# Local attention with memory and two MLPs on one core: slices of MLP 1's second weights in one tile and one request, values in two requests, and other places for loads and for the preparation of MLP 2's weights

## The chip, the cores and the metric

The kernel runs on one core of a Trainium2 chip. TensorE (PE in the rows) multiplies, and its weight loads (PEld) run beside the products. VectorE (DVE), ScalarE (ACT) and GpSimd (POOL) do the element-wise work. The DMA requests that matter here are issued by SyncE (SP) in the order in which its program lists them. The metric is the device time of one launch in microseconds (us).

## The reference

```python
# attention: batch 4, 8 heads, 768 positions, 64 per head; chunks of 32 queries
for c in range(24):
    k_full = concat([mem_k, k[chunk - 16 left : chunk + 8 right]])   # 8 memory keys + window
    v_full = concat([mem_v, v[same window]])
    out[chunk] = softmax(q[chunk] @ k_full.T / 8) @ v_full
x = out as [3072 tokens, 512]
# MLP 1: w_in [512, 2048], w_out [2048, 512]
h = x @ w_in;  g = h - tanh(h);  x = g @ w_out
# MLP 2: same shapes, other weights
h = x @ w_in
g = where(h >= 1, h, where(h <= -1, 0, (h + 1)**2 / 4));  out = g @ w_out
```

All inputs and the result are float32.

## The kernel before

**Number format.** Each float32 operand of a large product is split into a high and a low part in TensorE's own 32-bit format (fp32r), and three products are summed: high·high, low·high, high·low. So every weight slice exists twice, as `whi` and `wlo`, and every activation slice as `ghi` and `glo`. ScalarE makes a high part with a copy, VectorE the low part with a subtraction.

**Blocks.** The 3072 tokens are six blocks of 512 columns. The 2048 hidden units are sixteen slices (`FC`) of 128. A step `s` is one block and one slice: block `s // 16`, slice `s % 16`. `hidden(s)` (L706) makes `h` from twelve products of 512 columns, `gate(s)` (L716, L717) makes `g = h - tanh(h)`, and `output(s)` (L746) adds twelve products into the four banks of `acc` (two tiles, `acc0` and `acc1`, of two banks each). After a block's sixteen slices the four banks are copied to `y` (ScalarE copies `acc0`, VectorE copies `acc1`, L757) and stored in DRAM. The last two blocks run together in `both` (L784).

**Attention** is done in groups of eight chunks (`a`, L516 and L592), spread between the steps. Queries of a group come in one request, keys `k` in four, values `v` in four (L500).

**Weights of MLP 1.** They are loaded as float32 into `stage` (L159), rounded by ScalarE, VectorE and GpSimd, and split. The split second weights are written to DRAM once (`w1o_store`, L225, `hi` and `lo` apart) and read again for each later block (`w1o_load`, L234, also apart). Four pairs of tiles (`whi1_0` to `whi1_3` and the `lo` ones) take them in turn; blocks 2 and 3 use six homes.

**Weights of MLP 2** are prepared beside MLP 1: sixteen pieces (two weights, eight pieces each) pass through load, rounding (`prep_act`, L247 and L248, on ScalarE, then `prep_mag`, `prep_sign` and `prep_add` on VectorE), differences of quarters (`prep_sums`, L283, on VectorE), copies of the high parts (`prep_hi`, L297 and L310, on ScalarE), low parts (`prep_lo`, L316, on VectorE) and stores. `prep_items` lists these as items with a cost; `work(c)` is called after each product or step, adds `c` to a credit, and pops items until the credit is used up. So the costs and credits set at which product an item is issued.

**MLP 2's first layer** is done by Strassen's scheme in three parts of two blocks each (`early_plan(-2)`, `early_plan(-1)` and a last one). A product (`product`, L1069) is summed in PSUM in `qa`, `qb` or `qc`, and the results are combined through copies `u` and `v` (L972, ScalarE) and additions (L982, L1002, L1009, VectorE). A bank is used again only after its copy or addition has read it. The parts of weights that the products read come in requests at L961, ten of them ahead into homes named in the list `IN`.

**The order of the work** is a schedule written by hand: step `i` runs the lists `before`, `rounds`, `inside`, `between` and `behind`, and each engine executes its instructions in the order in which the program issues them. The stretches of the span are: the start to 48 us; hidden slices of block 0 to 107; outputs of blocks 0 and 1 to 258; `early_plan(-2)` to 342; outputs of blocks 2 and 3 to 457; `early_plan(-1)` to 535; `both` to 623; the last Strassen part of the first layer to 707; MLP 2's second layer (L1156) and what is left of the first to the end.

**SP's lanes.** Each request uses one of eight completion semaphores in turn (`DMAHW0` to `DMAHW7` in the kernel's order), and SP waits until that lane's request before has landed, so at most eight requests are under way.

Of the kernel before, what the change touches and what calls it, by code (L numbers as in the profile page):

```python
# [30 lines left out]
KC = DM // 128  # L31
# [48 lines left out]
def tile_memory_attention_two_mlps(  # L80
# [17 lines left out]
    att = ctx.enter_context(tc.tile_pool(name="att", bufs=2))  # L98
    ps_h = ctx.enter_context(tc.tile_pool(name="ps_h", bufs=2, space=PSUM))
# [100 lines left out]
    split_t = {}  # L200

    def split_weights_hi(s, which):
        phase, b, fc = steps[s]
        r = raw_t[phase, which, fc]
        hi = slot(f"whi{which}_{s % (W1O if which else 2)}", f"whi{which}_{s}", F32R)
# [3 lines left out]
    def split_weights_lo(s, which):  # L209
        phase, b, fc = steps[s]  # L210
        r, hi = raw_t[phase, which, fc], split_t[s, which]
        lo = slot(f"wlo{which}_{s % (W1O if which else 2)}", f"wlo{which}_{s}", F32R)
# [10 lines left out]
    def w1o_store(s):  # L223
        for i, t in enumerate(split_t[s, 1]):
            nc.sync.dma_start(out=w1o_d[steps[s][2]][:, i, :], in_=t.bitcast(F32))  # L225

    W1O_LATE = ("1_0", "1_1", "0_0", "0_1", "1_2", "1_3")

    def w1o_load(s):
        if s < PLAIN + FC:  # L230
            n = W1O_LATE[(s - NH) % 6] if NH <= s < PLAIN else f"1_{s % W1O}"
            t = [slot(f"w{w}{n}", f"w{w}1_{s}", F32R) for w in ("hi", "lo")]
            for i in range(2):
                nc.sync.dma_start(out=t[i].bitcast(F32), in_=w1o_d[steps[s][2]][:, i, :])  # L234
            split_t[s, 1] = t
# [160 lines left out]
    def prep_items():  # L396
# [8 lines left out]
        for n, p in enumerate(PAIRS):  # L405
# [6 lines left out]
                (1.4, [(load, n + 1, 0), (load, n + 1, 1), (prep_hi, *p, 0), (prep_sums, *p)]),  # L412
# [41 lines left out]
    def att_load(t, keys=True, values=True):  # L454
# [275 lines left out]
    def output(s):  # L730
# [80 lines left out]
    def retire(*tags):  # L811
# [6 lines left out]
        (-2, 7): ("whi1_2", "wlo1_2", "whi1_3", "wlo1_3"),  # L818
# [3 lines left out]
    def x_parts(sb, i):  # L822
        home = XHOME.get(i)
        name = f"xc{i}_{sb}"
        if (sb, i) in EARLY_HOME:
            home = EARLY_HOME[sb, i]
            if len(home) == 2:
                a = [wide.tile([128, 2, N], F32R, tag=tag, name=f"{name}_{k}") for k, tag in enumerate(home)]
# [549 lines left out]
    temps = ["ghi1", "glo1", "g14", "g15", "whi1_1", "wlo1_1"] + [f"y{i}" for i in range(KC)]  # L1378
# [132 lines left out]
```

## Time and profile before

| | us |
|---|---|
| median of three runs | 1094.72 |
| lowest and highest of them | 1092.56 and 1095.43 |
| the profiled execution | 1092.54 |
| its span (first to last instruction) | 1090.4 |
| around the span | 2.1 |

The profile's rows are one execution. A row of the timeline gives the start, the length, the engine, the line of the kernel, the operation, the tile written and the tile read, and, in brackets, how long the engine had been idle and what released it. A `q` behind an engine (SPq) is its sequencer, which issues requests. "PEclk" in a table by stretch is TensorE's granted clock as a share of 2.4 GHz (0.50 is 1.2 GHz), "DMA share" the mean busy share of the sixteen DMA engines.

### The profile page before, as it was taken

The page shows a single profiled execution, that of the slowest core. Times are in us where ns is not written, and L with a number is a line of the kernel's source. Part 1 is how long each engine was busy: PE and PEld are TensorE (multiplying, and loading weights), DVE is VectorE, ACT ScalarE, POOL GpSimd, SP SyncE. Part 2 cuts the span into 40 slices and gives each one's busy share as a digit, 9 for nine tenths or more (in the row PEclk, how much of TensorE's full clock was granted, in tenths as well). Part 3 has the DMA queues.
Part 4 walks back from the last instruction along what each step waited for, and adds up shares of the span by engine and source line. Part 5 has one row for each costly group of instructions (what it writes and reads, how often), then busy time and mean ns, then how long its engine had stood idle before and what let it go on. Part 6 is the DMA issues. An engine that isn't in the chain of part 4 may idle for free.

```text
span 1090.4 us, 20699 instructions
## 1 busy us (share of the span) xinstructions
PE 1050.5 (96%) x7535; PEld 849.1 (78%) x7541; DVE 821.7 (75%) x1384; ACT 639.6 (59%) x1164; POOL 42.6 (4%) x38
## 2 busy tenths in 40 slices
PE   7799999999889999999999999999999999999998
PEld 3577888777668877788788787788888888888887
DVE  4898978768887555677879988888567788476854
ACT  3588666436554332466546677756477756477653
POOL 0232221000000000000000000000000000000000
PEclk9899999999999999999999999999999999999999
DMA  9998986987867989799999898887866787767774
GB/s 215 257 258 223 263 234 200 281 235 247 279 230 211 265 242 283 271 325 344 375 342 297 282 362 280 261 265 217 250 195 192 224 260 220 226 194 194 202 204 147
DMA packets 218612, 274.01 MB, mean 251 GB/s; under 512 B 65808, under 2 KB 127504, under 8 KB 218512
## 3 DMA queue, kind: packets, MB, share of 16 engines
q1 hardware_dynamic: 218368, 272.57, 82.3%
q8 instruction: 60, 0.98, 0.4%
q14 instruction: 40, 0.33, 0.1%
q10 hardware_dynamic: 144, 0.13, 0.0%
HBM read 207.62 MB, written 65.01 MB: 250 GB/s over the span
## 4 chain that ended last, share of the span: by engine, by line
PE 81%; DVE 6%; DMA 5%; ACT 4%; SPq 3%; issue 1%; DVEq 0%; ACTq 0%
PE acc L1156 21%; PE acc L746 14%; PE qa L1069 10%; PE both L784 8%; PE h L706 7%; PE qc L1069 5%; PE qb L1069 2%; SPq L487 1%; PE a L592 1%; DMA stage<-w_in 1%; PE a L516 1%; DMA whi<-w1o 1%; SPq L500 1%; DMA wlo<-w1o 1%; ACT t L986 1%
## 5 line engine op out<-in xcount | busy, mean ns | idle before, releaser
L1156 PE MATMUL acc<-ghi,inG 128*128 128x512 f32 x672 | 183.0, 389 | 0.0
L288 DVE TENSOR_TENSOR glo<-g,ghi 128x512 fp32r<-128x512 f32 x194 | 130.0, 685 | 29.7 <-ACT ghi L287 27.9
L287 ACT ACTIVATE ghi<-g 128x512 fp32r<-128x512 f32 x194 | 118.6, 628 | 53.4 <-PE acc L1156 22.1
L1156 PEld LDWEIGHTS acc<-ghi,inG 128*128 128x128 f32 x672 | 126.2, 188 | 26.3
L1069 PE MATMUL qa<-xc,inP 128*128 128x512 f32 x576 | 141.2, 391 | 3.7 <-ACT u L972 2.5
L1069 PEld LDWEIGHTS qa<-xc,inP 128*128 128x128 f32 x576 | 107.3, 188 | 29.6 <-ACT u L972 5.5
L1156 PE MATMUL acc<-glo,inG 128*128 128x512 f32 x336 | 107.0, 389 | 0.0
L746 PE MATMUL acc<-ghi,whi 128*128 128x512 f32 x256 | 75.1, 406 | 5.3 <-DMA whi<-w1o 3.3
L1156 PEld LDWEIGHTS acc<-glo,inG 128*128 128x128 f32 x336 | 63.0, 188 | 13.4 <-DVE glo L288 0.5
L1069 PE MATMUL qc<-xc,inP 128*128 128x512 f32 x288 | 73.1, 389 | 0.0
L746 PE MATMUL acc<-ghi,wlo 128*128 128x512 f32 x256 | 70.9, 391 | 0.7 <-DMA wlo<-w1o 0.7
L746 PE MATMUL acc<-glo,whi 128*128 128x512 f32 x256 | 70.7, 390 | 0.0
L986 ACT ACTIVATE t<-g,half 128x512 f32<-128x512 f32 x58 | 42.0, 725 | 45.1 <-DVE g L982 45.1
L1069 PEld LDWEIGHTS qc<-xc,inP 128*128 128x128 f32 x288 | 54.0, 188 | 11.2
L746 PEld LDWEIGHTS acc<-ghi,whi 128*128 128x128 f32 x256 | 45.2, 188 | 16.5 <-DMA whi<-w1o 3.0
L746 PEld LDWEIGHTS acc<-ghi,wlo 128*128 128x128 f32 x256 | 47.9, 188 | 11.9 <-DMA wlo<-w1o 1.6
L987 ACT ACTIVATE t<-t 128x512 f32<-128x512 f32 x87 | 55.0, 632 | 2.8
L746 PEld LDWEIGHTS acc<-glo,whi 128*128 128x128 f32 x256 | 48.0, 188 | 10.5 <-issue 0.3
L194 POOL TENSOR_TENSOR raw<-raw,stage 128x512 int32<-128x512 int32 x32 | 41.9, 1309 | 144.1 <-DVE raw L189 88.5
L990 DVE SCALAR_TENSOR_TENSOR g<-t,g 128x512 f32<-128x512 f32 x58 | 39.7, 684 | 9.7 <-ACT t L987 9.7
L287 ACT ACTIVATE ghi<-s 128x512 fp32r<-128x512 f32 x46 | 28.7, 632 | 28.8 <-PE acc L1156 15.0
L706 PE MATMUL h<-xh,whi 128*128 128x512 f32 (+2 forms) x132 | 37.3, 404 | 5.3 <-DVE g L717 3.5
(1132 smaller groups left out, 2054.6 us busy)
## 6 DMA issues: line engine op xcount, KB each, us to landing
inP<-part SPq DMA_DIRECT2D x168, 256.0 KB, 3.1
inG<-part SPq DMA_DIRECT2D x168, 256.0 KB, 3.1
stage<-w_in SPq DMA_DIRECT2D x32, 512.0 KB, 5.9
stage<-w_out SPq DMA_DIRECT2D x32, 512.0 KB, 5.4
whi<-w1o SPq DMA_DIRECT2D x64, 256.0 KB, 5.0
wlo<-w1o SPq DMA_DIRECT2D x64, 256.0 KB, 5.8
k<-qkv_t SPq DMA_DIRECT2D x80, 128.0 KB, 5.2
v<-qkv_t SPq DMA_DIRECT2D x80, 128.0 KB, 4.0
```

Of the source, the lines that this page charges most:

```text
L194: eng.tensor_tensor(out=bits, in0=bits, in1=stage[:, :, 0], op=ALU.add)
L287: nc.scalar.activation(out=hi, in_=src, func=AF.Copy)
L288: nc.vector.tensor_tensor(out=lo, in0=src, in1=hi.bitcast(F32), op=ALU.subtract)
L487: nc.sync.dma_start(out=k[j // 2][:, j % 2], in_=ks[j, :, :, :WIN])
L706: nc.tensor.matmul(hp, w[:, kc * 128:(kc + 1) * 128], x[kc // 2][:, kc % 2, n0:n1], start=j == 0 and kc == 0, stop=j == 2 and kc == KC - 1,)
L746: nc.tensor.matmul(acc_t[dm], w[:, dm * 128:(dm + 1) * 128], g, start=first and j == 0, stop=last and j == 2,)
L784: nc.tensor.matmul(both_t[b, dm], w[:, dm * 128:(dm + 1) * 128], g, start=first and j == 0, stop=last and j == 2, skip_group_check=True,)
L986: nc.scalar.activation(out=t, in_=h, func=AF.Relu, scale=0.5, bias=half)
L987: nc.scalar.activation(out=t, in_=t, func=AF.Square)
L990: nc.vector.scalar_tensor_tensor(out=g, in0=t, scalar=1.0, in1=h, op0=ALU.min, op1=ALU.max)
L1069: nc.tensor.matmul(o, w[:, k * 128:(k + 1) * 128], z[k], start=i in (1, 2, 5) and j == 0 and k == 0, stop=j == 2 and k == 1, skip_group_ch ...
L1156: nc.tensor.matmul(bank[a][c], w[:, c * 128:(c + 1) * 128], g, start=first and j == 0, stop=last and j == 2, skip_group_check=True,)
```

## The change

**One tile and one request for a slice of the second weights.** `hi` and `lo` of a step are the two halves of one tile `w1_k` of 128 x 2 x 512, in a pool of its own. Store and load are one request of 512 KB in place of two of 256 KB. The six homes of blocks 2 and 3 are renamed; one of them, `0_0`, stays a pair of tiles with two requests. Some loads are issued earlier.

**Values in two requests.** A group's values come in two requests of 256 KB in place of four of 128 KB.

**Order.** At a block's first slice, the six products on `acc0` stand ahead of the six on `acc1`. In the preparation of MLP 2, `prep_sums` is an item ahead of the copy `prep_hi`, and the credits per product are other. The ten `IN` homes are other and loaded at other steps. Other tiles serve as spare ones in `early_plan`.

```diff
@@ slot
+        if tag[1:5] in ("hi1_", "lo1_"):
+            return w1p.tile([128, 512], dtype, tag=tag, name=name)
@@ w1o_store, w1o_load
-        for i, t in enumerate(split_t[s, 1]):
-            nc.sync.dma_start(out=w1o_d[steps[s][2]][:, i, :], in_=t.bitcast(F32))
-
-    W1O_LATE = ("1_0", "1_1", "0_0", "0_1", "1_2", "1_3")
+        nc.sync.dma_start(out=w1o_d[steps[s][2]], in_=w1_t[s].bitcast(F32))
+
+    HOMES = ("w1_0", "w1_1", "stage3", "0_0", "w1_2", "w1_3")
...
+        home = HOMES[(s - NH) % 6] if NH <= s < PLAIN else f"w1_{s % W1O}"
+        if home == "0_0":
+            t = [slot(f"w{w}0_0", f"w{w}1_{s}", F32R) for w in ("hi", "lo")]
             for i in range(2):
...
+        else:
+            t = (wide if home == "stage3" else w1p).tile([128, 2, 512], F32R, tag=home, name=f"w1_{s}")
+            nc.sync.dma_start(out=t.bitcast(F32), in_=src)
+            t = t[:, 0, :], t[:, 1, :]
+        split_t[s, 1] = t
@@ prep_items
-                (1.4, [(load, n + 1, 0), (load, n + 1, 1), (prep_hi, *p, 0), (prep_sums, *p)]),
+                (1.0, [(load, n + 1, 0), (load, n + 1, 1), (prep_sums, *p)]),
+                (0.4, [(prep_hi, *p, 0)]),
@@ att_load
-            att_v(t, (v[:, :NV // 2], v[:, NV // 2:]))
+            v = v.rearrange("p (j c) -> p j c", j=GC)
+            for u in range(2):
+                c = QK + u * 4 * D
+                nc.sync.dma_start(
+                    out=v[u * WIN:(u + 1) * WIN],
+                    in_=qkv[t * GC:(t + 1) * GC, :WIN, c:c + 4 * D].rearrange("j p c -> p j c"),
+                )
+            st[t]["v"] = [v[:, j] for j in range(GC)]
@@ output
+        if first:
+            products.sort(key=lambda p: p[1] // 2)
@@ IN
-    IN = ["whi0_0", "wlo0_0", "whi0_1", "wlo0_1", "raw1_0", "raw1_1", "raw1_2", "xn", "q0", "q1"]
-    for n in range(STREAM):
-        at_step(before, PLAIN + LAG - (3 if IN[n] in ("xn", "q0", "q1") else 9 - n), load_w, IN[n])
+    IN = (
+        ("raw1_0", 8), ("raw1_1", 7), ("raw1_2", 6), ("q0", 5), ("q1", 5), ("whi0_1", 4), ("wlo0_1", 4),
+        ("whi0_0", 3), ("wlo0_0", 3), ("xn", 2),
+    )
+    for tag, n in IN:
+        at_step(before, PLAIN + LAG - n, load_w, tag)
@@ ahead of and in early_plan(-2)
     w1o_load(NH)
+    w1o_load(NH + 1)
...
-        work(0.28)
+        if q < HALF - 1 or i == 1:
+            work(0.3)
@@ in early_plan(-1)
-        work(0.65)
+        if e[2] < HALF - 1 or e[3] == 1:
+            work(0.72)
         if e[2:] == (HALF - 2, 5):
-            w1o_load(PLAIN)
-            w1o_load(PLAIN + 1)
+            for fc in range(3):
+                w1o_load(PLAIN + fc)
@@ both's loop
-        if fc + 2 < FC:
-            w1o_load(PLAIN + fc + 2)
+        if fc + 3 < FC:
+            w1o_load(PLAIN + fc + 3)
```

What stands where is shown at three places. In these rows a number behind a tile's name is its running number in the program, and "x4" stands for four like requests in a row.

First, SP in the start, from the queries of attention group 4 to those of group 5. Before:

```order
L481 DMA q4_212<-qkv_t 128x4x128
L487 DMA k4_213<-qkv_t 128x4x64 x4
L500 DMA v4_219<-qkv_t 64x2x256 x4
L159 DMA stage_92<-w1_in 128x1024 x2
L159 DMA stage00_6_668<-w1_in 128x1024
L159 DMA stage00_7_692<-w1_in 128x1024
L481 DMA q5_694<-qkv_t 128x4x128
```

Now:

```order
L503 DMA q4_215<-qkv_t 128x4x128
L509 DMA k4_216<-qkv_t 128x4x64 x4
L481 DMA v4_222<-qkv_t 64x4x256 x2
L163 DMA stage_95<-w1_in 128x1024 x2
L163 DMA stage00_6_669<-w1_in 128x1024
L163 DMA stage00_7_693<-w1_in 128x1024
L503 DMA q5_695<-qkv_t 128x4x128
```

Two requests for `v4` stand ahead of the weights' stages where four stood.

Second, SP at the end of block 3, where the second weights of steps 58 to 62 and the first Strassen parts of `early_plan(-1)` (`inP_-1_...`) are loaded. Before:

```order
L234 DMA whi1_59_5707<-w1o11_131 128x512
L234 DMA wlo1_59_5708<-w1o11_131 128x512
L961 DMA inP_-1_0_1_5711<-part3_0_112 128x512
L234 DMA whi1_60_5744<-w1o12_132 128x512
L234 DMA wlo1_60_5745<-w1o12_132 128x512
L961 DMA inP_-1_1_1_5748<-part3_1_113 128x512
L234 DMA whi1_61_5801<-w1o13_133 128x512
L234 DMA wlo1_61_5802<-w1o13_133 128x512
```

Now:

```order
L244 DMA whi1_59_5558<-w1o11_134 128x512
L244 DMA wlo1_59_5559<-w1o11_134 128x512
L247 DMA w1_60_5593<-w1o12_135 128x1024
L986 DMA inP_-1_0_1_5595<-part3_0_115 128x512
L247 DMA w1_61_5648<-w1o13_136 128x1024
L986 DMA inP_-1_1_1_5650<-part3_1_116 128x512
L247 DMA w1_62_5672<-w1o14_137 128x1024
```

The load of step 60 is one request and stands ahead of the first Strassen part, which goes into `raw1_0`; before, that part went into `whi0_0` and stood ahead of step 60's loads.

Third, ScalarE at the end of `early_plan(-1)`, up to the first two high parts of `both` (`ghi_...<-g_0_...`). Before:

```order
L1006 ACTIVATE t_-1_6_21_6705<-qa-1_6_6563 128x512
L972 ACTIVATE u_-1_7_6715<-qa-1_7_6663 128x512
L310 ACTIVATE preph_6_3_6718<-prepr 128x256
L972 ACTIVATE v_-1_7_6730<-qc-1_7_6721 128x512
L297 ACTIVATE preph<-sums_6_6692 128x1024
L287 ACTIVATE ghi_6734<-g_0_6045 128x512
L287 ACTIVATE ghi_6738<-g_0_6133 128x512
```

Now:

```order
L324 ACTIVATE preph_6_3_6513<-prepr 128x256
L997 ACTIVATE u_-1_7_6525<-qa-1_7_6516 128x512
L311 ACTIVATE preph<-sums_6_6476 128x1024
L1031 ACTIVATE t_-1_6_12_6542<-g_13_6540 128x512
L1031 ACTIVATE t_-1_6_21_6554<-qa-1_6_6412 128x512
L997 ACTIVATE u_-1_7_6565<-qa-1_7_6516 128x512
L997 ACTIVATE v_-1_7_6577<-qc-1_7_6568 128x512
L301 ACTIVATE ghi_6579<-g_0_5888 128x512
L301 ACTIVATE ghi_6583<-g_0_5976 128x512
```

The copy `preph<-sums_6` stood directly ahead of the two high parts; it now stands five instructions earlier, ahead of the last two `t` copies of the piece before.

## Rows read from the trace of the kernel before

**Rows 1.** The page: engine, busy us (share of the span), instructions.

```profile
PE 1050.5 (96%) x7535; PEld 849.1 (78%) x7541; DVE 821.7 (75%) x1384; ACT 639.6 (59%) x1164; POOL 42.6 (4%) x38
```

**Rows 2.** Waits of PE: line and releaser, us in total, times, longest us.

```profile
PE h L706 <- DVE g L717: 3.5, 1, 3.5
PE acc L746 <- DMA whi<-w1o: 3.3, 4, 1.6
PE qa L1069 <- ACT u L972: 2.5, 6, 0.8
PE acc L746 <- DVE y L757: 2.0, 2, 1.0
...
PE both L784 <- ACT t_-1_7_11_6769 L1006: 1.9, 1, 1.9
PE a L592 <- DMA v<-qkv_t: 1.9, 1, 1.9
...
PE qa-2_5_4143 L1069 <- ACT u_-2_5_4197 L972: 1.6, 1, 1.6
...
PE acc L746 <- DMA wlo<-w1o: 0.7, 2, 0.5
PE qa-2_4_4034 L1069 <- ACT u_-2_4_4092 L972: 0.7, 1, 0.7
```

**Rows 3.** Stretch after 707 us: busy us of each engine (instructions), PEclk, DMA share, GB/s.

```profile
707.00:1090.00 383.00, 379.59 (x1674) 313.72 (x1672) 269.81 (x423) 236.16 (x392) 0.00 (x0) 1.00 0.73 214
```

**Rows 4.** SP's issues, 35 to 42 us: start us, us, engine line op out<-in xcount.

```profile
35.14 3.36 SPq L500 DMA_DIRECT2D v<-qkv_t  x4
38.62 3.29 SPq L159 DMA_DIRECT2D stage<-w_in  x4
```

**Rows 5.** Timeline of all engines, 43.5 to 48.6 us; in brackets idle before <-releaser.

```profile
43.78 0.66 ACT L171 ACTIVATE raw<-stage 128x512 f32<-128x512 f32 x1 [4.01 <-DMA stage<-w_in]
...
48.27 0.77 PE L706 MATMUL h<-xh,whi 128*128 128x512 f32 x1 [3.55 <-DVE g L717]
```

**Rows 6.** Stretches as in rows 3, around two PE waits.

```profile
38.00:40.00 2.00, 2.00 (x11) 1.65 (x11) 1.97 (x2) 1.23 (x2) 1.11 (x1) 1.00 0.69 145
48.00:52.00 4.00, 3.73 (x9) 2.88 (x10) 3.85 (x9) 4.00 (x19) 1.30 (x1) 0.50 0.92 203
419.00:421.00 2.00, 1.06 (x34) 0.61 (x41) 0.00 (x0) 0.00 (x0) 0.00 (x0) 1.00 0.89 233
```

**Rows 7.** SP's issues, 205 to 217 us.

```profile
205.94 3.34 SPq L500 DMA_DIRECT2D v<-qkv_t  x4
...
210.49 0.38 SPq L234 DMA_DIRECT2D whi<-w1o  x1
```

**Rows 8.** PE, 212 to 218 us.

```profile
216.93 1.20 PE L746 MATMUL acc<-ghi,whi 128*128 128x512 f32 x4 [1.61 <-DMA whi<-w1o]
```

**Rows 9.** SP's issues, 428 to 446 us.

```profile
429.76 0.40 SPq L234 DMA_DIRECT2D wlo<-w1o  x1
441.45 0.32 SPq L961 DMA_DIRECT2D inP_-1_0_1_5711<-part  x1
```

**Rows 10.** ACT, 525 to 538 us.

```profile
528.48 1.05 ACT L297 ACTIVATE preph<-sums 128x1024 fp32r<-128x1024 f32 x1
```

**Rows 11.** DVE, 525 to 538 us.

```profile
532.49 1.21 DVE L316 TENSOR_TENSOR prepl<-sums,preph 128x1024 fp32r<-128x1024 f32 x1
```

**Rows 12.** ACT, 623 to 626 us.

```profile
623.44 1.05 ACT L297 ACTIVATE preph<-sums 128x1024 fp32r<-128x1024 f32 x1
624.39 0.59 ACT L972 ACTIVATE u<-qa 128x512 f32<-128x512 f32 x1
```

**Rows 13.** The page's DMA issues: KB each, median us from issue to landing.

```profile
stage<-w_in SPq DMA_DIRECT2D x32, 512.0 KB, 5.9
...
whi<-w1o SPq DMA_DIRECT2D x64, 256.0 KB, 5.0
```

More of the change, by code (lines that the diff above doesn't have):

```diff
@@ L198, in round_rest @@
         round_sign(phase, which, fc)
-    split_t = {}
+    split_t, w1_t = {}, {}
     def split_weights_hi(s, which):
@@ L204, in split_weights_hi @@
         r = raw_t[phase, which, fc]
-        hi = slot(f"whi{which}_{s % (W1O if which else 2)}", f"whi{which}_{s}", F32R)
+        if which:
+            w1_t[s] = w1p.tile([128, 2, 512], F32R, tag=f"w1_{s % W1O}", name=f"w1_{s}")
+            hi = w1_t[s][:, 0, :]
+        else:
+            hi = slot(f"whi0_{s % 2}", f"whi0_{s}", F32R)
         nc.scalar.activation(out=hi, in_=r, func=AF.Copy)
@@ L211, in split_weights_lo @@
         r, hi = raw_t[phase, which, fc], split_t[s, which]
-        lo = slot(f"wlo{which}_{s % (W1O if which else 2)}", f"wlo{which}_{s}", F32R)
+        lo = w1_t[s][:, 1, :] if which else slot(f"wlo0_{s % 2}", f"wlo0_{s}", F32R)
         nc.vector.tensor_tensor(out=lo, in0=r, in1=hi.bitcast(F32), op=ALU.subtract)
@@ L223, in w1o_store @@
     def w1o_store(s):
-        for i, t in enumerate(split_t[s, 1]):
-            nc.sync.dma_start(out=w1o_d[steps[s][2]][:, i, :], in_=t.bitcast(F32))
-    W1O_LATE = ("1_0", "1_1", "0_0", "0_1", "1_2", "1_3")
+        nc.sync.dma_start(out=w1o_d[steps[s][2]], in_=w1_t[s].bitcast(F32))
+    HOMES = ("w1_0", "w1_1", "stage3", "0_0", "w1_2", "w1_3")
     def w1o_load(s):
-        if s < PLAIN + FC:
-            n = W1O_LATE[(s - NH) % 6] if NH <= s < PLAIN else f"1_{s % W1O}"
-            t = [slot(f"w{w}{n}", f"w{w}1_{s}", F32R) for w in ("hi", "lo")]
-            for i in range(2):
-                nc.sync.dma_start(out=t[i].bitcast(F32), in_=w1o_d[steps[s][2]][:, i, :])
-            split_t[s, 1] = t
+        if s >= PLAIN + FC:
+            return
+        src = w1o_d[steps[s][2]]
+        home = HOMES[(s - NH) % 6] if NH <= s < PLAIN else f"w1_{s % W1O}"
+        if home == "0_0":
+            t = [slot(f"w{w}0_0", f"w{w}1_{s}", F32R) for w in ("hi", "lo")]
+            for i in range(2):
+                nc.sync.dma_start(out=t[i].bitcast(F32), in_=src[:, i, :])
+        else:
+            t = (wide if home == "stage3" else w1p).tile([128, 2, 512], F32R, tag=home, name=f"w1_{s}")
+            nc.sync.dma_start(out=t.bitcast(F32), in_=src)
+            t = t[:, 0, :], t[:, 1, :]
+        split_t[s, 1] = t
     def prep_load(w, q):
@@ L827, in x_parts @@
             if len(home) == 2:
-                a = [wide.tile([128, 2, N], F32R, tag=tag, name=f"{name}_{k}") for k, tag in enumerate(home)]
+                pool = w1p if home[0] == "w1_2" else wide
+                a = [pool.tile([128, 2, N], F32R, tag=tag, name=f"{name}_{k}") for k, tag in enumerate(home)]
                 t = [a[k // 2][:, k % 2, :] for k in range(4)]
@@ L1377, in tile_memory_attention_two_mlps @@
         step(i)
-    temps = ["ghi1", "glo1", "g14", "g15", "whi1_1", "wlo1_1"] + [f"y{i}" for i in range(KC)]
+    temps = ["ghi1", "glo1", "g14", "g15"] + [f"y{i}" for i in range(KC)]
     spare.extend(temps)
     w1o_load(NH)
+    w1o_load(NH + 1)
     pairs_out(0)
@@ L1411, in tile_memory_attention_two_mlps @@
     pairs_out(1)
-    temps = [f"w{w}1_{i}" for i in (2, 3) for w in ("hi", "lo")] + [f"g{w}{i}" for i in (1, 2) for w in ("hi", "lo")]
+    temps = [f"g{w}{i}" for i in (1, 2) for w in ("hi", "lo")] + ["g14", "g15", "raw0_14", "raw0_15"]
+    temps += [f"y{i}" for i in range(KC)]
     spare.extend(temps)
```

16 lines of the change are left out of this document (11 added, 5 removed).

## The prediction

> **What bounds the kernel now.** I read the page's busy times first. TensorE is busy 96% of the span, VectorE, the next, 75% [rows 1]. So a gain can only come from TensorE's remaining waits, and the next view is the table of them [rows 2]. It has to be read by place. After 707 us TensorE is busy 379.6 of 383 us [rows 3]; no wait in the table belongs there, and the change moves nothing that TensorE waits for there. What is left falls into four kinds. One wait in the start: 3.5 us for a `g` of VectorE. Waits for second weights and values, which SP issues: 3.3 (four), 0.7 (two) and 1.9 us, together 5.9. Two waits of 1.0 us for the copies `y` at a block's end. And waits for VectorE or ScalarE at the Strassen products: seven named ones at `early_plan(-2)`, from 1.6 down to 0.7, that sum to 8.1, one of 1.9 at `both`, and six that sum to 2.5 after 623 us. The two `-2` rows shown are the longest and the shortest of the seven.
>
> The instructions on TensorE, VectorE, ScalarE and GpSimd are the same in number. Only SP's list is shorter: 40 requests fewer for values (20 groups, four to two), 16 fewer stores and 59 fewer loads of second weights, 115 in all. The bytes are the same. So each part below asks one question: which wait ends earlier.
>
> **A, the start.** SP takes 3.36 us to issue the four requests of `v4`, 0.84 each, and only then the next weight stage, at 38.62 [rows 4]. Its landing releases ScalarE at 43.78, after 4.01 us of idleness, and five VectorE steps later TensorE goes on at 48.27, after 3.55 us [rows 5]. With two requests the stage is issued 1.7 us earlier if a request of double size costs SP the same (bounds: 0 to 2.2, since the DMA engines have room, share 0.69 at 38 to 40 us [rows 6]). I take 1.6 off the wait, bounds 0 and 2.2.
>
> The same wait has a second price: the granted clock is 0.50 from 48 to 52 us [rows 6], so TensorE runs at 1.2 GHz after it. Half of some 5.5 us is about 2.8 us. After a wait of 1.85 us at 419.83 the clock stayed 1.00 [rows 6], so a wait of about 2 us may leave it alone here too. Between 2.8 and 0 I take 1.9, since the shortened wait is nearest to that row, with some doubt. A gives 1.6 + 1.9 = 3.5, between 0 and 5.0.
>
> **B, the copies.** At a block's first slice TensorE has two products for `acc0`, then needs `acc1`, which VectorE is still copying; that costs 1.0 us twice [rows 2]. Now six products on `acc0` stand ahead. A product takes 0.23 us, from the 1.20 us of four of them with a last one of 0.4 or so [rows 8], so four more cover 0.9. They need the low parts earlier; VectorE makes `glo` of that slice ahead of the copies in either order, and the low weight comes with the high one. B gives 2 x 0.9 = 1.8, between 1.0 and 2.0.
>
> **C, second weights and values.** At 216.93 TensorE waits 1.61 us for a slice [rows 8] whose request SP issued at 210.49, right behind four requests of `v14` that took 3.34 us, and two stages [rows 7]. Two requests in place of four put it 1.7 us earlier; the hi part then shares a landing with the lo part. At 419.83 (1.85 us) it waits for values that stand behind the same kind of queue. Near 445 us the cause is another: SP stood from 429.76 to 441.45 at a Strassen part that went into `whi0_0`, and the loads of steps 60 to 63 were queued behind it [rows 9]. Now that part goes to `raw1_0`, and step 60's load stands ahead of it. All this is 5.9 us [rows 2]. I take three quarters, 4.4, because each load still has to land and the DMA share at 419 to 421 is 0.89 [rows 6]; bounds 0.5 and 5.9.
>
> Here a page speaks against the change. First the row: on this trace issuing is not small, 3.34 us for four requests against a landing some 5 us after issue [rows 7, 13]. The Trainium skill, "DMA: Bandwidth & Descriptors", section "Issuing engines are not separate DMA queues", says that the time on the sequencer to start a DMA is usually small relative to the DMA itself. By that rule A and C would give next to nothing, and the sum would be 7.9 us smaller; the result is the first rival below. The trace does not agree with it at these two places, since the late request there is late by SP's queue.
>
> **D, `early_plan(-2)`.** The seven waits are for copies `u` and `v` of ScalarE that stand behind preparation work. The credits and items move: in places ScalarE's rounding goes behind a `t` that is waited for (about 0.7 better), a block of VectorE differences of 128 x 512 now stands ahead of an addition that is waited for (about 0.9 worse), and low parts leave the last products (about 1 better). No row shows the new order. I take 0, bounds 2 better and 2 worse, from moving one or two of the seven waits of 0.7 to 1.6.
>
> **E, the start of `both`.** The first products wait 1.9 us [rows 2] for a chain of additions. It was held up on ScalarE by the copy of the differences, 1.05 us at 528.48 [rows 10], and on VectorE by their low part, 1.21 us at 532.49 [rows 11]. Both stand earlier now, behind work that TensorE does not wait for. E gives 1.4, with bounds of 2.1 better and 1.0 worse, since the preparation in `early_plan(-1)` is denser (0.72 for 0.65) and that stretch has no wait in the table now.
>
> **F, MLP 2's first layer after 623 us.** Typical is 623.44: a copy `preph<-sums` of 1.05 us stands ahead of the `u` for which TensorE waits [rows 12]. In the new order most `u` copies stand ahead of such copies, but at 625 us three copies `preph` stand in front of it too, which may cost about 0.9. From six waits, 2.5 us [rows 2], and some of VectorE's, I take 1.2, bounds 2.5 better and 2.0 worse.
>
> **The sum.** 3.5 + 1.8 + 4.4 + 0 + 1.4 + 1.2 = 12.3 us. The profiled execution took 1092.54, so it becomes 1080.2. That execution is 2.18 under the median of the runs, 1094.72, as one of three; the median becomes 1082.4.
>
> **The rivals.**
>
> *The DMA engines and not SP set the landings.* Then A and C bring little: earlier requests only wait longer in the engines. For it speaks a share of 0.89 at the very wait for values [rows 6], against it 0.69 at the start and that SP's queue and TensorE's wait fit so closely in length. B, E and F remain: 4.4 us, 1090.3. A clock that still falls in the start is a half of this, 1084.3.
>
> *The moved preparation takes its time back.* D and E and F come out at their bad ends: 2.0 + 1.0 + 2.0 lost in place of 2.6 won, 7.6 worse than the forecast, 1090.0. For it speaks that the credits only move ScalarE's and VectorE's work and remove none; against it, that each wait of [rows 10 to 12] names one copy, and that copy is moved.
>
> *Slower: a slice's first product waits for 512 KB.* Before, the high part landed by itself after 5.0 us; a request of 512 KB takes 5.9 [rows 13]. So TensorE can start a step 0.9 us later if SP issues the load no earlier. This happens at 59 loads. It decides from 14 late loads on: 14 x 0.9 = 12.6 us eats the forecast's gain; at 20 it is 18, and the time is 1100.4. Against it: four waits for high parts in 64 loads [rows 2] say that most loads have slack, and SP's issue of the pair is a step shorter. By the Trainium skill, "DMA: Bandwidth & Descriptors", section "Anatomy of one DMA — SWDGE (gpsimd) path", a request takes about 2.0 us and its bytes at 436 GB/s, which for 256 KB more is an estimate of 0.6 us; the sum by that would be 20 x 0.6 = 12 us, 1094.4. The rows' 0.9 stands in the sum.
>
> *It doesn't do what it says.* If SP is held by the eight lanes, a request of double size holds its lane longer, and SP ends where it was. All but B is then lost: 1092.9.
>
> **How the numbers follow.** The forecast, within some 4 us: 0.58. DMA-bound, in whole or by the clock alone beyond that: 0.16. Preparation takes it back: 0.12. It doesn't do what it says: 0.07. Slower: 0.07. A measurement of this kernel can tell about 0.3%, 3.3 us, from no change; faster means under 1091.4, slower over 1098.0. Forecast, DMA-bound and preparation lie under 1091.4, less about a quarter of the latter two (their bad ends): 0.79 faster. With the fourth case and that quarter, 0.14 same; 0.07 slower. The range goes down to the favourable bounds of A, C, D, E and F, 1.5 + 1.5 + 2.0 + 0.7 + 1.3 = 7.0 us below, 1075.4, and up past the first two rivals, 1091.5.
>
> **What would show each step.** In the changed kernel's profile: A, the first stage of four issued near 37.0 in place of 38.62, the wait at 48 us near 2 us, and PEclk 1.00 from 48 to 54. B, no or short waits for `y`. C, the rows of `w1` and `v` gone from TensorE's waits, and no gap of SP before 441. D, a sum of `u` and `v` waits at `early_plan(-2)` of 6 to 10 us. E, the wait at `both` under 0.6. F, the sum after 623 us under 2.5. The forecast is wrong if PEclk still falls and the waits for `w1` remain (first rival), or if new waits for `u`, `v` or `g` appear (second), or if waits for `w1` come at many steps (third).

## The result and the profile after

The changed kernel took 1100.21 us (median of five runs, 1098.72 to 1103.02) against 1094.72 for the kernel before (1092.56 to 1095.43). The ratio is 1.0057, with a 95% interval of 1.0037 to 1.0076: it is slower by 0.57%. 1082.4 was forecast. Its profiled execution took 1100.95 us, with a span of 1099.1.

The page first: TensorE is as busy in share as before [rows 1], with the same number of weight loads (7541), but 8.3 us longer in time.

```profile
PE 1058.8 (96%) x7541; PEld 849.8 (77%) x7541; DVE 821.7 (75%) x1384; ACT 639.6 (58%) x1164; POOL 42.7 (4%) x38
```

The table of TensorE's waits (line and releaser, us in total, times, longest us) answers to [rows 2]:

```profile
PE qa L1094 <- ACT u L997: 5.5, 6, 1.7
PE acc L770 <- DMA w<-w1o: 3.1, 1, 3.1
...
PE qa-2_4_3951 L1094 <- ACT u_-2_4_4003 L997: 2.1, 1, 2.1
PE qa L1094 <- DVE g L1015: 1.9, 3, 1.0
PE h L728 <- DVE g L739: 1.9, 1, 1.9
...
PE qa-1_7_6516 L1094 <- ACT u_-1_7_6565 L997: 1.0, 1, 1.0
...
PE qa-1_1_5867 L1094 <- ACT u_-1_1_5990 L997: 0.7, 1, 0.7
```

The waits for `y`, for values and at `both` are gone, as foretold. The start's wait fell from 3.5 to 1.9. But the waits of `qa` (after 623 us) rose from 2.5 to 5.5 and those for a `g` of the second kind from 0.9 to 1.9, one wait for second weights is now 3.1 us, and two new ones stand in `early_plan(-1)`.

This does not sum to the loss. The next view is the start of the first product of each stretch, from TensorE's timelines of both kernels. A stretch runs from there to the first product of the next, so a wait ahead of a first product counts in the stretch before it. The lengths of the stretches in us:

| stretch | before | after | difference |
|---|---|---|---|
| start to the first output product | 107.1 | 105.4 | -1.7 |
| outputs of blocks 0 and 1 | 147.2 | 151.7 | +4.5 |
| `early_plan(-2)` | 87.0 | 87.7 | +0.7 |
| outputs of blocks 2 and 3 | 115.6 | 111.2 | -4.4 |
| `early_plan(-1)` | 78.7 | 79.2 | +0.5 |
| `both` | 87.1 | 89.2 | +2.1 |
| first layer of MLP 2, last Strassen part | 79.8 | 85.3 | +5.5 |
| the rest, to TensorE's end | 384.1 | 384.3 | +0.2 |

`both` is the line that no step of the prediction holds. The wait of 1.9 us ahead of it counts in `early_plan(-1)`, and in `both` itself TensorE has no wait in either kernel's table; still it takes 2.1 us longer. What is in it shows in a stretch without waits. Here are 60 us of `both` and 60 us of a later stretch (busy us of each engine with its instructions, PEclk, DMA share, GB/s), before:

```profile
540.00:600.00 60.00, 60.00 (x266) 49.69 (x265) 52.46 (x81) 32.72 (x54) 0.00 (x0) 1.00 0.96 322
780.00:840.00 60.00, 60.00 (x266) 49.70 (x265) 37.44 (x58) 40.85 (x68) 0.00 (x0) 1.00 0.71 203
```

and after:

```profile
540.00:600.00 60.00, 60.00 (x260) 48.64 (x259) 49.86 (x78) 30.91 (x52) 0.00 (x0) 1.00 0.90 305
780.00:840.00 60.00, 60.00 (x266) 49.69 (x265) 35.63 (x55) 38.07 (x64) 0.00 (x0) 1.00 0.73 211
```

TensorE is busy all the time at the full granted clock in all four rows. Before, 266 products touch the 60 us; after, 260 in `both`, and 266 again later. From start to start that is 226.7 ns a product before (the mean of the 167 of `both` that start between 562 and 600 us) and 232.3 ns after (164 products); 384 products of `both` at 5.6 ns more make 2.15 us, an estimate that is the whole difference. About the same (232.5 ns on the average) stands in the outputs of blocks 0 to 3 where the weights come from one of the new tiles `w1_k`; in the steps with weights from `whi0_0` and `wlo0_0`, the home that stayed, the median is 227 to 228 in the same trace. In the `both` of the kernel before, the weights lay in `whi1_k` and `wlo1_k`.

Where the tiles lie is listed in the compiled programs. Before, all tiles of 2 KB that TensorE reads start at 704 bytes past a multiple of 2048. After, the pool of the new tiles was opened behind the pool `att`, which holds four tiles of 32 bytes, so `w1_0` to `w1_3` start at 832, 128 bytes off all others.

### The profile page after: what moved, and what is told of

It reads as the page before. It is cut to its first block, busy times and chain, and to the rows that moved or that the text cites. A ratio compares the mean times of both kernels' runs of the same rounds, so it can differ in the third digit from the quotient of the medians.

```text
span 1099.1 us, 20601 instructions
## 1 busy us (share of the span) xinstructions
PE 1058.8 (96%) x7541; PEld 849.8 (77%) x7541; DVE 821.7 (75%) x1384; ACT 639.6 (58%) x1164; POOL 42.7 (4%) x38
## 4 chain that ended last, share of the span: by engine, by line
PE 78%; DVE 7%; ACT 5%; DMA 4%; SPq 3%; issue 2%; DVEq 0%; ACTq 0%
PE acc L1181 20%; PE acc L770 15%; PE qa L1094 9%; PE both L808 8%; PE h L728 7%; PE qc L1094 4%; PE qb L1094 2%; SPq L509 1%; PE a L614 1%; DVE g L1027 1%; DMA stage<-w_in 1%; PE a L538 1%; DVE g L1007 1%; DMA part<-first 1%; DMA w<-w1o 1%
## 5 line engine op out<-in xcount | busy, mean ns | idle before, releaser
L770 PE MATMUL acc<-ghi,w 128*128 128x512 f32 x472 | 126.3, 405 | 3.2 <-DMA w<-w1o 3.1
L770 PEld LDWEIGHTS acc<-ghi,w 128*128 128x128 f32 x472 | 87.2, 191 | 24.0 <-DMA w<-w1o 3.4
L770 PE MATMUL acc<-glo,w 128*128 128x512 f32 x236 | 67.2, 398 | 0.0
L808 PE MATMUL both<-ghi,w 128*128 128x512 f32 x256 | 65.6, 395 | 0.0
L808 PEld LDWEIGHTS both<-ghi,w 128*128 128x128 f32 x256 | 48.2, 188 | 11.2
L770 PEld LDWEIGHTS acc<-glo,w 128*128 128x128 f32 x236 | 45.0, 191 | 10.7
```

The lines of the kernel that those rows point to most:

```text
L770: nc.tensor.matmul(acc_t[dm], w[:, dm * 128:(dm + 1) * 128], g, start=first and j == 0, stop=last and j == 2,)
L808: nc.tensor.matmul(both_t[b, dm], w[:, dm * 128:(dm + 1) * 128], g, start=first and j == 0, stop=last and j == 2, skip_group_check=True,)
```

## The experiments

Times of kernels are compared by their ratio to the kernel before in the same series on the same chip. The kernel before had medians of 1092.7 to 1094.9 in the four series, and most intervals are some 0.15 to 0.2% wide to each side, about 2 us.

### The place of the new tiles

The changed kernel with the pool of the small tiles opened first, so that all other tiles shift together (all of them then start at 832):

```diff
     const = ctx.enter_context(tc.tile_pool(name="const", bufs=1))
+    att = ctx.enter_context(tc.tile_pool(name="att", bufs=2))
...
-    att = ctx.enter_context(tc.tile_pool(name="att", bufs=2))
     slices = tc.tile_pool(name="slices", bufs=1)
```

> The changed kernel with one line moved: the pool of the attention's 32-byte tiles is opened first, so that the new tiles w1_k and the activations ghi and glo lie at like addresses again (the same distance modulo 2048 bytes), as the second weights did in the kernel before. In the changed kernel the new tiles lie 128 bytes off, and each product that reads weights from them takes 232.3 ns from start to start; those from other tiles, and all of the kernel before, take 226.7. Theory 'place in memory': the pitch goes back to 226.7 ns in both and in the outputs; some 1100 products times 5.6 ns is 6.2 us less than the changed kernel, about 1094. Rival 'the form of the tile or the 512 KB request slows the reads': the pitch stays at 232 ns and the time at 1100.

Measured: 1094.91 us, ratio 1.0009 (0.9993 to 1.0026), 5 us less than the changed kernel. The 60 us of `both`:

```profile
540.00:600.00 60.00, 60.00 (x266) 49.69 (x265) 49.93 (x76) 31.01 (x52) 0.00 (x0) 1.00 0.90 314
```

266 products again, 226.7 ns each, and `both` takes 87.1 us. The theory of the place holds. The reverse, on the kernel before:

```diff
     att = ctx.enter_context(tc.tile_pool(name="att", bufs=2))
+    w1p = ctx.enter_context(tc.tile_pool(name="w1p", bufs=1))
...
+        if tag[1:5] in ("hi1_", "lo1_"):
+            return w1p.tile([128, 512], dtype, tag=tag, name=name)
         return slots.tile([128, 512], dtype, tag=tag, name=name)
```

> The kernel before, with one thing changed: the second weights' eight tiles (whi1_k, wlo1_k, each apart as before, two requests each) come from a pool of their own behind the 32-byte tiles, so that they lie 128 bytes off the other tiles' step. Theory 'place in memory': products from them take 232.3 ns for 226.7; 11 of 12 steps use them, some 1000 products times 5.6 ns is 5.6 us, the time is about 1100. Rival 'form of the tile or request': nothing changes, 1094.7.

Measured: 1096.95 us, ratio 1.0025 (1.0008 to 1.0043).

```profile
540.00:600.00 60.00, 60.00 (x260) 48.65 (x259) 52.71 (x82) 31.52 (x53) 0.00 (x0) 1.00 0.92 312
```

260 products, 232.4 ns each, with separate tiles and separate requests: neither the form of the tile nor the request of 512 KB is the cause. The loss is 2.7 us and not 5.6, though `both` alone is 2.2 us longer in the traces (89.3 for 87.1). Where the rest went was not shown. Part of the slower pitch in the outputs may lie where TensorE would have waited for a request anyway: the stretch of blocks 2 and 3 took 114.1 us, not more than before's 115.6.

How far off is too far was asked later, on the changed kernel with the preparation as before:

```diff
+    pad = ctx.enter_context(tc.tile_pool(name="pad", bufs=1))
+    pad.tile([128, 96], F32, tag="pad", name="pad")
     slices = tc.tile_pool(name="slices", bufs=1)
```

> The changed kernel with the preparation as before and 384 bytes of unused space ahead of the new tiles: they lie 512 bytes off the others' step in place of 128. Theory 'only a distance that is no multiple of 512 bytes is slow' (a product's weights are 512 bytes of a tile's row): products take 226.7 ns and the time is near 1090. Rival 'any distance is slow, it is the multiple of 2048 that counts': 232 ns and 1095.

Measured: 1089.38 us, ratio 0.9953 (0.9934 to 0.9971).

```profile
540.00:600.00 60.00, 60.00 (x265) 49.63 (x265) 49.94 (x77) 30.13 (x50) 0.00 (x0) 1.00 0.92 316
```

265 products, 226.8 ns from start to start: 512 bytes off is as good as none (0.9955 with none, the run with both undone below), 128 bytes off is not. Other distances were not tried.

### The preparation

The changed kernel with the items and the credits of before:

```diff
-                (1.0, [(load, n + 1, 0), (load, n + 1, 1), (prep_sums, *p)]),
-                (0.4, [(prep_hi, *p, 0)]),
+                (1.4, [(load, n + 1, 0), (load, n + 1, 1), (prep_hi, *p, 0), (prep_sums, *p)]),
...
-        if q < HALF - 1 or i == 1:
-            work(0.3)
+        work(0.28)
...
-        if e[2] < HALF - 1 or e[3] == 1:
-            work(0.72)
+        work(0.65)
```

> The changed kernel with the preparation of MLP 2's weights listed as before: the copy of the first high part ahead of the differences in one item of cost 1.4, and credits of 0.28 and 0.65 at every product. Theory 'the moved preparation took the time after 623 us': TensorE's waits there fall from 8.3 us to about 4 and the time by 4 to 6 us, to about 1095. Rival 'those waits come from the other spare tiles or from the loads': they stay at 8 us and the time at 1100.

Measured: 1094.96 us, ratio 1.0018 (1.0003 to 1.0033), 4 us less than the changed kernel by the ratios. The stretch after 623 us is back at 79.9 us. `early_plan(-2)` became 0.7 us longer (88.4), and the wait of 1.9 us at `both` came back.

Both undone at once:

> The changed kernel with the attention's small tiles opened first (so that the new tiles lie in step) and the preparation listed as before, both together. Theory 'two separate losses': the gains of the two single runs, 5.3 and 5.2 us, add up: 1089.7 us, 4 to 5 under the kernel before; products at 226.7 ns, waits after 623 us near 3.7 us. Rival 'what is left is worth nothing': 1094 as the kernel before.

Measured: 1089.73 us, ratio 0.9955 (0.9935 to 0.9975): 5 us faster than the kernel before. The two losses are separate and add up within their intervals (5.2 and 4.3 us alone, 11.2 together, by the ratios), and what is left of the change is a gain. The waits of this run after 610 us are those of before:

```profile
PE qa L1093 <- ACT u L996: 2.4, 6, 0.8
PE qa L1093 <- DVE g L1014: 0.9, 1, 0.9
PE qa L1093 <- DVE g L1006: 0.3, 1, 0.3
```

How the loss comes about can be read in the changed kernel. ScalarE, then TensorE, at the first product of that stretch:

```profile
625.38 0.71 ACT L324 ACTIVATE preph<-prepr 128x256 fp32r<-128x256 f32 x2
625.99 1.04 ACT L311 ACTIVATE preph<-sums 128x1024 fp32r<-128x1024 f32 x1
626.94 0.58 ACT L997 ACTIVATE u<-qa 128x512 f32<-128x512 f32 x1
```

```profile
627.58 1.66 PE L1094 MATMUL qa<-xc,inP 128*128 128x512 f32 x6 [1.67 <-ACT u L997]
```

Three copies `preph` and the copy of the differences stand in front of the `u` that TensorE waits for. Before, at this place, only the copy of the differences did [rows 12]. The credits had moved the preparation half a piece on, so that other items were in turn at 625 us and later. At 673 us three copies `preph` stand ahead of a `u` again (a wait of 1.05 us). At other places it is VectorE's part of the preparation, as here at the end of the stretch:

```profile
703.21 1.22 DVE L330 TENSOR_TENSOR prepl<-sums,preph 128x1024 fp32r<-128x1024 f32 x1 [1.51 <-ACT preph L311]
705.06 0.72 ACT L1011 ACTIVATE t<-g,half 128x512 f32<-128x512 f32 x1 [1.89 <-DVE g L1007]
708.23 0.97 PE L1094 MATMUL qa<-xc,inP 128*128 128x512 f32 x3 [1.49 <-ACT u L997]
```

A low part of 1.22 us stands ahead of the addition `g` (704.35), ScalarE idles for 1.89 us until it has it, and the `u` behind ScalarE's `t` copies comes late.

Which of the parts does it was asked with four runs on the version with both undone. First the order of the items alone:

> The run with both undone, with the differences again an item of 1.0 ahead of the copy of 0.4, and the old credits. Theory 'the order of the items makes the waits after 623 us': they sum to 7 or 8 us for 3.5, and the time is 4 to 5 us over that run's 1089.7. Rival 'the credits make them, by leaving another item in turn at 620 us': the waits stay at 3.5 and the time at 1090.

Measured: 1091.14 us, ratio 0.9974 (0.9954 to 0.9993). The waits after 623 us sum to 4.6 us for 3.6, not to 7 or 8, so the order alone doesn't make them. The stretch takes 81.0 us, `early_plan(-1)` 80.0. Then both credits, with the old items:

> The run with both undone, with the old items and the new credits (0.30 and 0.72, none in the last products). Theory 'the order of the items makes the waits after 623 us': those waits stay near 3.5 us and the time near 1090. Rival 'the credits make them': waits of 7 to 8 us and 1094.

Measured: 1090.75 us, ratio 0.9970 (0.9950 to 0.9989). The waits after 610 us:

```profile
PE qa L1093 <- ACT u L996: 4.4, 6, 1.5
PE qa L1093 <- DVE g L1014: 1.7, 2, 1.0
```

The stretch takes 83.5 us, 3.6 more than with the old credits. The waits are near the rival's 7 us, the time is not near its 1094: `early_plan(-2)` is 1.2 us shorter (87.4) and the wait at `both` is gone, so most of it is paid back. Then each credit alone:

> The run with both undone, with the new credits in early_plan(-2) alone (0.30, none in the last products). Theory 'each stretch pays or gains by its own credits': the waits from 258 to 342 us fall from 9 to 7 us, nothing changes after 535 us, and the time falls by 1 to 2.5 us, to 1087 to 1089. Rival 'the first credits shift all that follows': the waits after 623 us rise by 3 us and the time to 1091 or more.

> The run with both undone, with the new credits in early_plan(-1) alone (0.72, none in the last products). Theory 'these credits make the waits after 623 us': the wait of 1.9 us at the start of both goes, waits of 6 to 7 us for 3.5 stand after 623 us, and the time is 1 us or more over 1089.7. Rival: the waits after 623 us stay at 3.5 us and the time falls by 1.5 us.

Measured: 1095.49 us (ratio 1.0016, 1.0001 to 1.0031) and 1094.29 us (1.0011, 0.9997 to 1.0025). The stretch after 623 us takes 84.9 and 83.8 us. The theory that each stretch has its own credits fell: credits in `early_plan(-2)` change what happens 300 us later (waits of 6.5 us for 3.6). The theory on the credits of `early_plan(-1)` held in kind: the wait at `both` is gone, the waits after 623 us sum to 5.8 us, and the time is up. In that stretch the order alone costs 1.1 us, the first credit 5.0, the second 3.9, both credits 3.6, all three 5.5, so the parts don't add. Nor do they in the time: against the run with both undone, by the ratios, the order alone costs some 2 us, either credit alone 6 to 7, both credits 1.6, all three 6 (the run with the tiles in step). The waits of each setting name other copies and additions; which of them meet is decided anew each time.

### Requests: the number, the merging, the order

The changed kernel with values in four requests:

```diff
-            v = v.rearrange("p (j c) -> p j c", j=GC)
-            for u in range(2):
...
+            att_v(t, (v[:, :NV // 2], v[:, NV // 2:]))
```

> The changed kernel with the values of a group in four requests of 128 KB again. Theory 'SP's issuing sets the landings': the start's wait at 47 us grows from 1.9 to 3.5 us, the waits for values near 420 us come back, and the time rises by 3 to 5 us, to about 1104. Rival 'the DMA engines set the landings': the slice that TensorE waits for at 217 us lands when it did, and the time stays within 1 us of 1100.

Measured: 1098.19 us, ratio 1.0049 (1.0031 to 1.0068), 0.1% under the changed kernel, which its interval can't tell from it; the theory's 3 to 5 us more didn't come. So it was asked again on the version with both undone:

> The run with both undone, with the values of a group in four requests of 128 KB. Theory 'the DMA engines set the landings': the slice that TensorE waits for near 215 us lands within 1 us of where it did, and the time stays within 1.5 us of 1089.7. Rival 'SP's issuing sets them' (the prediction's step A and C): the wait in the start grows by 1.7 us, and the time to 1093 or more.

Measured: 1089.37 us, ratio 0.9964 (0.9948 to 0.9981), the same as with two requests (0.9955). The first output product stands at 104.8 us in both profiles, and the start's wait didn't grow: 2.2 us with four requests, 2.5 with two. Two requests in place of four are worth nothing that these runs can measure; up to some 3 us could hide in the intervals of one such pair. One thing in the profiles stays open: in both runs with four, TensorE has a wait near 410 us of 3.1 and 2.5 us, for which the profile shows no releaser, and a lower clock behind it; in their partners with two it is 1.0 and 1.3, and the stretch of blocks 2 and 3 is 4.5 and 3.3 us shorter. The medians don't show it.

Loads of second weights in two requests, into the same tiles:

```diff
-            nc.sync.dma_start(out=t.bitcast(F32), in_=src)
             t = t[:, 0, :], t[:, 1, :]
+            for i in range(2):
+                nc.sync.dma_start(out=t[i].bitcast(F32), in_=src[:, i, :])
```

> The run with both undone, and the loads of second weights in two requests of 256 KB again (high part first), into the same tiles. Theory 'a slice's first product waits for 512 KB': the wait near 214 us falls from 3.0 to 1.6 us or less and the time by 2 to 4 us. Rival 'the queue ahead of it sets the landing': the wait stays near 3 us and SP's longer list costs 1 to 2 us elsewhere.

Measured: 1089.40 us, ratio 0.9955 (0.9939 to 0.9971), no difference. TensorE's wait near 214 us:

```profile
214.79 1.63 PE L770 MATMUL acc<-ghi,w 128*128 128x512 f32 x4 [2.97 <-DMA w<-w1o]
```

It is 2.97 us for 3.08 us with one request. The slower rival of the prediction, that a first product waits for 512 KB at 14 loads or more, is out. Its 1100.4 us lies next to the measured 1100.21 by luck: the changed kernel has one wait for a slice in its table.

The products of a block's first slice in the old order:

```diff
-        if first:
-            products.sort(key=lambda p: p[1] // 2)
```

> The run with both undone, and the products of a block's first slice in the old order. Theory: the two waits of 1.0 us for the copies y come back near 200 and 400 us, and the time rises by 1.8 us. Rival: the waits that follow (for a slice near 214 us) become shorter by as much, and the time rises by 0.9 or less.

Measured: 1088.15 us, ratio 0.9948 (0.9929 to 0.9967), not slower. The two waits in question in this run:

```profile
199.84 1.65 PE L767 MATMUL acc<-ghi,w 128*128 128x512 f32 x6 [1.01 <-DVE y L778]
...
217.03 1.19 PE L767 MATMUL acc<-ghi,w 128*128 128x512 f32 x4 [2.44 <-DMA w<-w1o]
```

The wait for `y` is back at 1.01 us, and the next one, for a slice, is 0.6 us shorter and, unlike the 3.08 us with the sorted order, not followed by a lower clock (1.00 for 0.57 from 216 to 220 us).

The Strassen parts of `early_plan(-1)` in their old homes and order:

> The run with both undone, and the ten Strassen parts of early_plan(-1) in their old homes and order. Theory 'SP stood behind a part that waited for its home': SP stands for some 10 us before 445 us again, the waits there (1.0 and 0.5 us) come back, and the time rises by 1.5 to 2 us. Rival: the loads of second weights are ahead in any case, no wait appears, 0.

Measured: 1097.42 us, ratio 1.0022 (1.0006 to 1.0038), 7 us more than with the new order; 2 were expected. SP, then TensorE, in this run:

```profile
425.23 0.42 SPq L244 DMA_DIRECT2D wlo<-w1o  x1
443.58 0.32 SPq L985 DMA_DIRECT2D inP_-1_0_1_5562<-part  x1
```

```profile
448.10 2.47 PE L769 MATMUL acc<-ghi,w 128*128 128x512 f32 x5 [4.55 <-DMA w<-w1o]
```

SP stands for 18 us, where it stood 12 in the kernel before [rows 9], and TensorE waits 4.55 us. The profiled stretch of blocks 2 and 3 takes 115.7 us for 110.4; besides, the granted clock is 0.90 in the four us around the wait at `both` and 0.67 in the next four, which was 1.00 in the run with the new order. Without this part nothing of the change's gain is left (1.0022 for 0.9955). The 7 us are the price of the old order among the other changes, where SP stands longer, and not what the kernel before lost by it.

Last, an attempt at the wait near 215 us, on the run with the old order of the first slice: the stores of `y` at the ends of blocks 0 and 2 one step later.

```diff
...
-                nc.sync.dma_start(out=y_t[b][:, dm, :], in_=y)
+                y_late.append((y_t[b][:, dm, :], y))
+            if b not in (0, 2):
+                y_stores()
...
+        y_stores()
         run(behind, i)
```

> The run with the first slice's products in the old order, with the four stores of y at the ends of blocks 0 and 2 issued one step later, behind that step's loads. Theory 'the queue that SP builds up behind the stores of y sets the landing near 215 us': the loads that stood behind them are issued some 3 to 5 us earlier, while the DMA engines have room, the wait of 2.4 us there falls under 1 and the time by 2 us or more. Rival 'the DMA engines are the limit from 200 to 217 us, whatever comes first': the wait stays over 2 us and the time at 1088.

Measured: 1089.20 us, ratio 0.9951 (0.9935 to 0.9966), no gain. The wait is 1.78 us for 2.44, at 216.95 us. The three slices are issued from 209.13 us on, and from 208.78 without the edit: it didn't bring them forward, so its theory was not tested. It stays open what would end the wait; that the queue of requests from 200 us on is more than the DMA engines pass by then fits all runs, and was not shown by itself.

The earlier loads of second weights and the other spare tiles were not tried alone.

## Why the prediction was wrong, point by point

**What was not in the sum at all.** The prediction held that the change leaves TensorE's instructions alone and asked only which wait ends earlier. It took the time of a product as given, and so put this term at nothing without a reason. The new tiles lie 128 bytes off, and each product from them takes 5.6 ns more; in the profiles `both`, where TensorE waits in neither kernel, lost 2.1 us by it. Undone, it is 5 us of 1100. The order of instructions shows nothing of this, and the profile of the kernel before can't; the list of addresses in the compiled program, which was there, would have raised the question, not the price.

**A, the start: wrong, its size met by luck.** The stage was issued at 36.70 for 38.62 and TensorE's wait fell from 3.55 to 1.86 us, near what was worked out. But the landing didn't follow the issue. ScalarE, which the stage releases, went on at 42.87 for 43.78, 0.9 us earlier for 1.9 us of issue, and the other half of the shorter wait is that TensorE came to it 0.8 us later. The two runs that differ in these requests alone show it. With two requests (both undone):

```profile
36.03 6.02 SPq L163 DMA_DIRECT2D stage<-w_in  x4
42.83 0.67 ACT L175 ACTIVATE raw<-stage 128x512 f32<-128x512 f32 x1 [2.91 <-DMA stage<-w_in]
```

With four:

```profile
38.63 3.52 SPq L163 DMA_DIRECT2D stage<-w_in  x4
42.64 0.67 ACT L175 ACTIVATE raw<-stage 128x512 f32<-128x512 f32 x1 [2.62 <-DMA stage<-w_in]
```

Issued 2.6 us earlier, the stage released ScalarE 0.2 us later. (In the other pair, the changed kernel and the same with four: issued 1.6 us earlier, 0.1 later.) That SP's issue sets this landing is the step that failed; the first rival held here. For room in the DMA engines I had read their share with four requests, 0.69 at 38 to 40 us [rows 6]. With the requests issued earlier the engines are fuller earlier: in this pair the share from 36 to 40 us is 1.06 with two and 0.79 with four, and from 40 to 44 us 0.99 and 0.93. (The share counts the packets that start in a stretch with their whole time, so it can pass 1.00.)

The clock fell too, for a shorter time. Before, from 52 us, and after, from 48 and from 52:

```profile
52.00:54.00 2.00, 2.00 (x9) 1.67 (x7) 1.69 (x4) 0.84 (x2) 0.11 (x1) 0.54 0.88 259
```

```profile
48.00:52.00 4.00, 4.00 (x15) 3.06 (x13) 3.80 (x9) 3.84 (x14) 1.30 (x1) 0.59 1.14 204
52.00:54.00 2.00, 2.00 (x70) 1.44 (x69) 1.75 (x4) 1.55 (x3) 1.00 (x1) 0.96 1.04 288
```

The granted clock is 0.59 after a wait of 1.86 us, where I had inferred 1.00 from one row [rows 6]; in the run with both undone it stayed at 1.00 from 48 to 52 us after a wait of 2.47. So the length of the wait didn't decide it. And the first output product's place, 107.1 us before and 105.4 after, is within what one execution differs from another: over the four profiles with four requests it lies between 103.9 and 107.1, over the thirteen with two between 103.3 and 110.1. The term was chosen from a single execution's start, 3.5 us of a stretch that scatters by as much. By the Trainium skill ("DMA: Bandwidth & Descriptors", "Issuing engines are not separate DMA queues"), against which I had set the rows, the time on the sequencer is usually small relative to the DMA. The runs agree with it here: halving the requests is worth nothing (0.9955 with two, 0.9964 with four).

**B, the copies: right in mechanism, worth nothing.** Both waits are gone in the changed kernel. The run without the sorting shows where the gain went: into the next wait, for a slice that lands when it lands. (The row that the prediction names gives 0.27 us a product; 0.23 is what other rows give. Nothing hangs on it.)

**C, second weights and values: half right.** Near 445 us the cause was named rightly and its size was too small: the stretch of blocks 2 and 3 fell from 115.6 to 110.4 us with the other losses undone, and undoing the order costs 7 us. While SP stood, the DMA engines of the kernel before moved nothing:

```profile
435.00:440.00 5.00, 5.00 (x26) 4.14 (x25) 1.11 (x3) 1.56 (x5) 0.00 (x0) 1.00 0.00 0
```

At 217 us the step failed. SP issued the slice 1.85 us earlier, as foretold:

```profile
208.64 2.00 SPq L247 DMA_DIRECT2D w<-w1o  x3
```

It landed at 217 us as before [rows 8], and TensorE, which was earlier, waited longer and lost its clock:

```profile
212.00:216.00 4.00, 1.92 (x13) 1.45 (x11) 2.72 (x7) 2.04 (x6) 0.00 (x0) 1.00 1.02 395
216.00:220.00 4.00, 2.97 (x7) 2.39 (x8) 0.86 (x2) 0.41 (x1) 0.00 (x0) 0.50 1.04 275
```

With four requests in the changed kernel the same slice was issued 1.1 us later and landed 1.0 us earlier:

```profile
209.74 1.34 SPq L247 DMA_DIRECT2D w<-w1o  x3
216.08 3.35 PE L763 MATMUL acc<-ghi,w 128*128 128x512 f32 x7 [2.19 <-DMA w<-w1o]
```

So SP's issue doesn't set this landing either. The share of 1.02 at 395 GB/s fits DMA engines that are full, and is the row to look for. I had taken the share at another wait, 0.89 at 419 us, for this one. The first rival held here, and not near 445.

**D, `early_plan(-2)`: right in size.** The forecast was 0, within 2; the stretch took 87.7 for 87.0 us. Its parts were not taken from any row.

**E, the start of `both`: right at its place, paid back beside it.** The wait of 1.9 us is gone; two new ones of 0.7 and 1.0 stand in `early_plan(-1)`, and the stretch, which holds all three, took 79.2 us for 78.7. In place of a gain of 1.4 that is a loss of 0.5, within the bound of 1.0 on the bad side. The denser preparation had been named as the risk.

**F, MLP 2's first layer: wrong in sign.** 1.2 us of gain were forecast, the stretch lost 5.5. I had read the order of single copies and judged each by the wait that it stood near. The extra 0.9 at 625 us was seen, and it came: 1.67 for 0.76. But preparation also came to stand ahead of other products, on ScalarE at 673 us and on VectorE at 686, 697 and 708 us (waits of 0.96, 0.79 and 1.49), and I took those for better without a row. That is the step that failed: the moved preparation was counted as moved out of the way. The bound of 2.0 on the bad side was set from the size of the old waits; nothing tied the new ones to it. The second rival, that the moved preparation takes its time back, was the right one; by its price, 7.6 us, it would have given 1090.0.

In sum: the rival on preparation, the DMA rival at two places, and a cause that was on no list came together.

## What to carry to other kernels

Before a pool is opened at another place, or tiles of another form, compare the addresses of the operands that TensorE reads at the same time, and after the run count the products in a stretch without waits: a pitch that changes by 2% shows in no wait. An order that is set by credits or costs is not moved in one place; every item after it meets other partners, so the waits that a stretch has don't bound its price: 5.5 us were lost where 3.7 us of waits had stood. Before a request that is issued earlier is taken to land earlier, read the share of the DMA engines between the two times at that very place: here it was 1.06 and 1.02 in the runs where the earlier issue didn't help, and 0.00 before the change where the new order did. And a term from the start of one execution should be held against how much starts differ.

The version with the new tiles in step, the preparation as before and the first slice in the old order took 1088.15 us, 0.9948 (0.9929 to 0.9967) of the kernel before; it is the fastest by its median, though the others near it (0.9951 to 0.9955) can't be told from it.

## What the runs showed of the hardware

TensorE's pitch depends on where weights and activations lie to each other: 226.7 ns for a product of 512 columns with all tiles in step or 512 bytes off, 232.3 or 232.4 ns with the weights 128 bytes off, in the four traces with them there, at the full granted clock. Why it is so was not shown.

A wait of the same length can cost the clock or not. TensorE's wait of 1.9 us at the start of `both` is in twelve of the traces. In seven of them, the kernel before among them, the clock stays at 1.00; in five it falls. Before, the four us around the wait and the four after it:

```profile
534.00:538.00 4.00, 2.40 (x11) 2.01 (x12) 3.84 (x7) 2.68 (x5) 0.00 (x0) 1.00 1.06 399
538.00:542.00 4.00, 4.00 (x19) 3.34 (x18) 3.46 (x5) 3.34 (x5) 0.00 (x0) 1.00 1.08 375
```

In the run with loads in two requests:

```profile
527.00:531.00 4.00, 2.10 (x6) 1.43 (x5) 3.84 (x7) 2.31 (x5) 0.00 (x0) 0.79 1.06 389
531.00:535.00 4.00, 4.00 (x15) 3.19 (x15) 3.85 (x6) 3.62 (x5) 0.00 (x0) 0.78 1.05 395
```

TensorE has no other wait in the table of `early_plan(-1)` ahead of it in either, and `both` took 87.1 us in the one and 89.4 in the other; of these 2.3 us the clock makes 1.7, an estimate from the two shares. So near 2 us of a single profile can be this alone. What decides it was not shown.
